# Attention scans into PSUM banks, fillers into the next product's bank, and a planner that counts the shared port

## The chip, the cores and the metric

One core of a Trainium2 chip runs the whole program. TensorE (PE; its weight loads are PEld) multiplies, VectorE (DVE), ScalarE (ACT) and GpSimd (POOL) do the element work, and SyncE (SP) issues most of the transfers. SBUF is the working memory; PSUM, eight banks of 2 KB per partition, takes the products of TensorE. The metric is the device time of one execution in microseconds (us), lower is better; a kernel's time is the median of its runs.

## What is computed

Three layers in fp32, cut to the core:

```python
# layer 1: gated linear attention, 4 x 8 heads, 768 steps, head size 48
for t in range(S):
    state = alpha[:, :, t, :, None] * state + k[:, :, t] (outer) v[:, :, t]
    y[:, :, t] = q[:, :, t] @ state
x = y as [3072 tokens, 384]
# layer 2: 8 experts, each token goes to its two best
noisy = x @ w_gate + log1p(exp(x @ w_noise)) * noise
out[token] = sum over its top 2 of weight * (relu(x @ w1[e]) @ w2[e])     # 384 -> 1024 -> 384
# layer 3: dense, leaky relu
h = out @ w_in;  result = max(0.01 * h, h) @ w_out                        # 384 -> 2048 -> 384
```

## The kernel before

**Order of the work.** No engine's order is written out by hand. `build_unit`, `build_route` and `build_experts` register steps with a `Planner` (line 70): the engine (or two to choose from), an estimated duration, what the step depends on, which buffers it takes (`Ring`s, listed at line 923 with their sizes) and a due time. `prepare` hands due times back from each step to those it waits for. `run` (line 125) keeps a clock for each engine, always issues the step that can start first by these estimates, and breaks ties by the due time. Each engine then executes its instructions in that order. `run(1)` issues until the attention is done, with phase 1 steps alone; `run(2)` issues the rest.

**Attention** goes in 24 units of 128 steps, all heads at once (`build_unit`, line 932), six units for each of the four sequences. SP loads `at` (alpha), `kq` and `nv`. On DVE `back` (line 963) scans alpha backwards into `suf` with one long scan, `forth` (969) scans forwards into `wt` in two halves, each behind a small reciprocal; then `keys` (988) multiplies k by `suf` into `kt` and `queries` (992) q by `wt` into `qp`. `suf` and `wt` lie in SBUF, three buffers each. The scans' second operand, a pattern of resets, lies in a PSUM bank `pC` (line 909). POOL multiplies the totals of alpha (`total`, 978). On TensorE `turn_k` (1000) transposes the keys into a `pM` bank, ACT copies them out (1004), `update` (1048) and `carry` (1052) add up the new state in another `pM` bank, ACT copies it to `S` (1057), and POOL decays it for the next unit (`sp`, 1039). `score` (1013) writes two banks, ACT copies them (1017), POOL masks them (1022), `within` (1069) and `across` (1076) make y in `pY`, ACT copies it (1093), and `turn_y` (1098) transposes y and multiplies by the gate weights into a `pA` bank, from which ACT copies x (1102) and DVE takes the logits (1107). The eight banks in this stage: `pA` 2, `pC` 1, `pM` 2, the scores 2, `pY` 1.

**Fillers.** Where the planner sees TensorE idle for more than 0.45 us ahead of a product, `keep_busy` (line 917) issues matmuls of the identity, so many as fit into the gap. They write to the unused end of bank `pC`.

**Routing.** After four units (one group of 512 tokens, six groups) some thirty small steps on DVE and ACT (`gate_top2`, line 177, and `build_route`, 1121) find each token's two experts and its slot, and POOL scatters the rows of x to the slots in DRAM (`x_s`), eight indirect transfers for a group (line 1191). The first two experts' first rows (`EARLY`) need groups 0 to 3 alone.

**Experts and dense layer** (`build_experts`, 649). Each product is split into three fp32r products of high and low parts. Weights come by SP and are split by ACT (`split_hi`, 464) and by DVE or POOL, whichever the planner finds free (`split_lo`, 468). Rows are loaded from `x_s` (526), transposed by TensorE into `pA` (`turn`, 600) and split by ACT (604) and DVE (609). `gemm1` (742) writes `ph`, `gemm2` (781) adds up in `py`.

Of the kernel before, what the change touches and what calls it, by code (L numbers as in the profile page):

```python
# [16 lines left out]
DRAM = bass.MemoryType.DRAM  # L17

SQ_MAX, TOT_MIN = 460.0, 1e-14
PERIOD = 6.0  # L20
RDUE = -10.0
# [6 lines left out]
RGROUPS = ((0,), (1,), (2,), (3,), (4,), (5,))  # L28
CAP = G0 + G1
GROUP2 = 384  # L30
F64B = 2
XGB = 11
# [37 lines left out]
class Planner:  # L70

    NEAR, FAR, SLACK, RATE, LAND = 0.1, 0.25, 0.8, 0.26, 2.0
    GAP, FILL, COLD, AHEAD, MARGIN = 0.45, 0.24, 0.45, 0.3, 3.0

    def __init__(self):
        self.steps, self.free, self.dma = [], dict.fromkeys("pavgs", 0.0), 0.0
        self.filler = None

    def add(self, eng, dur, fn, deps=(), use=(), takes=(), phase=1, due=1e9, lat=0.0, size=0):

        deps = list(deps)
        st = Step(eng, dur, fn, deps, list(takes), phase, due, lat, size)
        for owner, ring in use:
            deps.append(owner)
            owner.holders[ring].append(st)
        for ring in st.takes:
            ring.planned.append(st)
        self.steps.append(st)
        return st

    def prepare(self):
# [13 lines left out]
        for st in sorted(self.steps, key=lambda x: -order[x]):  # L105
            for nx in st.succ + [x for x in before.get(st, []) if order[x] > order[st]]:
                far = 0 if nx.eng == st.eng else self.SLACK
                st.due = min(st.due, nx.due - nx.longest() - far - st.lat)
        self.waiting = set(self.steps)
        self.open = [st for st in self.steps if not st.left]  # L110

    def start_of(self, st):
        t = 0.0
        for d in st.deps:
            t = max(t, d.end + (self.NEAR if d.used == st.eng[0] else self.FAR))
        for ring in st.takes:
# [8 lines left out]
    def run(self, phase, until=None):  # L125

        left = set(until) if until else None
        while left or (left is None and any(s.phase <= phase for s in self.waiting)):
            best = {}
            for st in self.open:  # L130
# [5 lines left out]
                for e in st.eng:  # L136
                    t0 = max(t, self.free[e])
# [12 lines left out]
            if e == "p" and self.filler and t0 - self.free[e] > self.GAP:  # L150
                self.filler(int((t0 - self.free[e]) / self.FILL if self.free[e] else (t0 - 1.0) / self.COLD))
# [3 lines left out]
            self.free[e] = t0 + dur  # L155
            st.t0 = t0
# [20 lines left out]
def gate_top2(nc, work, lg, noise, desc, n, tagp, res):  # L177
# [28 lines left out]

    @op(A)
    def _():
        nc.scalar.activation(t3("ln"), flat(t["u"]), AF.Ln)

    @op(V)
    def _():
        nc.vector.scalar_tensor_tensor(t3("um"), flat(t["u"]), -1.0, flat(t["ex"]), op0=OP.add, op1=OP.subtract)
# [122 lines left out]
def tile_kernel(  # L336
# [50 lines left out]
    ps2 = fctx.enter_context(tc.tile_pool(name="psum2", bufs=2, space=PSUM))  # L387
# [129 lines left out]
    scattered, late, taken = [], [], []  # L517
# [5 lines left out]
    def load_rows(e, g, j):  # L523
# [3 lines left out]
        if g == 0 and e < EARLY:  # L527
# [62 lines left out]
    XT, XP = {}, {}  # L590

    def turn(key, j):
# [5 lines left out]
        p = XP[key, j] = ps2.tile([128, KD, 128], FT, name="pA")  # L598
# [50 lines left out]
    def build_experts(t0, R, scat, last_x, ready_at, totals, acc_done, begun):  # L649
# [18 lines left out]
        def turned(key, phase):  # L668
            done = []
            for j, (o, n) in enumerate(blocks(key)):  # L670
                own = [XO[key]] if j else []
                w = add("p", 0.34, lambda j=j: turn(key, j), own + AUX.get((key, j), []),
                        use=[(GX[key + (j,)], R["xg"])] + [(x, R["XT"]) for x in own],
                        takes=[R["pA"]] + ([] if j else [R["XT"]]), phase=phase, due=tm[0] - 7 + 0.8 * j if phase == 2 else 1e9)
                if not j:
                    XO[key] = w
                hi = add("a", 0.5, lambda j=j: turned_hi(key, j), use=[(w, R["pA"]), (XO[key], R["XT"])], phase=phase)
                lo = add("v", 0.57, lambda j=j: turned_lo(key, j), [hi], use=[(w, R["pA"]), (XO[key], R["XT"])], phase=phase)
# [4 lines left out]
        def expert_weights(i, after):  # L683
# [4 lines left out]
            for m, nm in enumerate(("w1s", "w2s")):  # L688
# [175 lines left out]
        for si, (gi, f, nf) in enumerate(steps):  # L864
# [31 lines left out]
            if si == first[2 * EARLY]:  # L896
                v0 = add("v", 1.3, violations, totals, phase=2, due=tm[0] + 40)
# [6 lines left out]
    with ExitStack() as actx:  # L904
# [5 lines left out]
        scb, warm = bank[:PP, 0:HB * C + C], bank[:, HB * C + C:]  # L910
# [6 lines left out]
        def keep_busy(n):  # L917
            for _ in range(n):
                nc.tensor.matmul(warm, identf, identf, start=True, stop=True)  # L919

        plan.filler = keep_busy
# [560 lines left out]
```

## Time and profile before

| | us |
|---|---|
| median of 3 runs | 1096.68 (1092.26 to 1100.07) |
| the profiled execution | 1087.71 |
| its span, first to last instruction | 1085.9 |
| TensorE busy, of the span | 1042.8 |
| VectorE busy | 593.7 |
| ScalarE busy | 388.2 |
| GpSimd busy | 278.5 |

All rows below are of the profiled execution, and their times count from the start of its span. Busy times are averages over stages of different kinds: the attention lies at the front, and the experts and the dense layer fill the rest.

### The profile page before, as it was taken

Reading aid. Unit: us, or ns where it says so; the run is one execution under the profiler, and the core shown is the slowest. Engines: PE = TensorE matmul, PEld = TensorE weight load, DVE = VectorE, ACT = ScalarE, POOL = GpSimd, SP = SyncE. Lnnn points to the kernel's source line nnn. Section 1 sums busy time; section 2 is a strip of 40 time slices with the busy share of each in tenths; the row PEclk is TensorE's granted clock in tenths of the full one; section 3 lists DMA queues with packets and bytes.
Section 4 is the critical chain, followed back from the end, with each engine's and each line's share of the span. In section 5 each row is a group of like instructions: output and inputs, shape, how many; then the busy total and the mean of one; then the engine's idle time right before and its main releaser. Section 6 shows DMA issues by size and latency. Waiting matters only on the chain.

```text
span 1085.9 us, 18172 instructions
## 1 busy us (share of the span) xinstructions
PE 1042.8 (96%) x6839; PEld 999.2 (92%) x6839; DVE 593.7 (55%) x1218; ACT 388.2 (36%) x825; POOL 278.5 (26%) x321
## 2 busy tenths in 40 slices
PE   6999895999999999999999999999999999999997
PEld 5887775999999999999999989899999999999997
DVE  5998997223464565646574233455554545454543
ACT  3755644223354544445453222222222222212211
POOL 3466876200032253424351021410110100000000
PEclk9998997999999999999999999999999999999999
DMA  9667746413464565746567344320101100000000
GB/s 232 203 203 242 237 129 222 157 50 103 148 201 141 179 200 164 226 142 207 180 222 241 116 153 139 92 66 9 59 22 45 34 33 16 22 1 23 1 22 26
DMA packets 78917, 133.20 MB, mean 123 GB/s; under 512 B 8514, under 2 KB 56260, under 8 KB 78820
## 3 DMA queue, kind: packets, MB, share of 16 engines
q1 hardware_dynamic: 72292, 111.89, 33.2%
q0 software_dynamic: 6528, 20.06, 5.7%
q8 instruction: 56, 0.92, 0.4%
q14 instruction: 41, 0.34, 0.1%
HBM read 93.38 MB, written 38.54 MB: 121 GB/s over the span
## 4 chain that ended last, share of the span: by engine, by line
PE 87%; DVE 8%; issue 2%; DMA 1%; ACT 1%; another core or an unknown queue 1%; POOL 0%; DVEq 0%; ACTq 0%; POOLq 0%
PE py L781 39%; PE ph L742 39%; PE pA L600 2%; DVE wt L974 1%; PE pS L1013 1%; DVE suf L965 1%; PE pA L1098 1%; PE pY L1069 1%; PE pC L919 1%; PE pY L1076 1%; DVE kt L988 1%; PE pM L1048 1%; DMA xg<-y_d,gidx 1%; DVE g_z L225 0%
## 5 line engine op out<-in xcount | busy, mean ns | idle before, releaser
L766 DVE SCALAR_TENSOR_TENSOR hl<-ph,hh 128x384 fp32r<-128x384 f32 (+1 forms) x128 | 77.4, 606 | 192.3 <-ACT hh L759 186.1
L752 ACT ACTIVATE hc<-ph 128x384 f32<-128x384 f32 x128 | 63.0, 492 | 300.6 <-PE ph L742 283.3
L755 DVE SCALAR_TENSOR_TENSOR hc<-hc 128x384 f32<-128x384 f32 x128 | 71.4, 558 | 178.2 <-ACT hc L752 178.2
L759 ACT ACTIVATE hh<-ph 128x384 fp32r<-128x384 f32 (+1 forms) x128 | 68.0, 532 | 241.7 <-PE ph L742 236.0
L781 PE MATMUL py<-w2hA,hh 128*128 128x384 f32 (+1 forms) x416 | 141.5, 340 | 1.1 <-issue 1.1
L781 PE MATMUL py<-w2hB,hh 128*128 128x384 f32 (+1 forms) x416 | 141.9, 341 | 0.2 <-issue 0.2
L781 PE MATMUL py<-w2lB,hh 128*128 128x384 f32 (+1 forms) x416 | 140.5, 338 | 0.4 <-issue 0.4
L781 PE MATMUL py<-w2hB,hl 128*128 128x384 f32 (+1 forms) x416 | 140.5, 338 | 0.0
L781 PE MATMUL py<-w2hA,hl 128*128 128x384 f32 (+1 forms) x416 | 140.0, 337 | 0.0
L781 PE MATMUL py<-w2lA,hh 128*128 128x384 f32 (+1 forms) x416 | 139.9, 336 | 0.0
L742 PE MATMUL ph<-xh,w1hA 128*128 128x384 f32 (+1 forms) x384 | 136.4, 355 | 1.4 <-ACT hc L752 0.7
L742 PE MATMUL ph<-xl,w1hA 128*128 128x384 f32 (+1 forms) x384 | 134.3, 350 | 1.0 <-issue 1.0
L742 PE MATMUL ph<-xh,w1hB 128*128 128x384 f32 (+1 forms) x384 | 134.1, 349 | 0.4 <-DVE hl L766 0.4
L742 PE MATMUL ph<-xh,w1lA 128*128 128x384 f32 (+1 forms) x384 | 134.1, 349 | 0.0
L742 PE MATMUL ph<-xl,w1hB 128*128 128x384 f32 (+1 forms) x384 | 133.4, 347 | 0.0
L742 PE MATMUL ph<-xh,w1lB 128*128 128x384 f32 (+1 forms) x384 | 133.3, 347 | 0.0
L804 POOL DMA_INDIRECT xg<-y_d,gidx x48 | 46.5, 968 | 279.6 <-PE pA L600 172.7
L781 PEld LDWEIGHTS py<-w2lA,hh 128*128 128x128 f32 (+1 forms) x416 | 77.3, 186 | 2.2 <-issue 1.2
L781 PEld LDWEIGHTS py<-w2lB,hh 128*128 128x128 f32 (+1 forms) x416 | 77.6, 187 | 1.3 <-issue 0.3
L781 PEld LDWEIGHTS py<-w2hB,hh 128*128 128x128 f32 (+1 forms) x416 | 77.5, 186 | 0.8
L769 DVE TENSOR_TENSOR hl<-hc,hh 128x384 fp32r<-128x384 f32 x128 | 71.4, 558 | 12.3 <-DVE hh L761 0.5
L781 PEld LDWEIGHTS py<-w2hB,hl 128*128 128x128 f32 (+1 forms) x416 | 77.6, 187 | 0.5 <-issue 0.5
(160 smaller groups left out, 1877.3 us busy)
## 6 DMA issues: line engine op xcount, KB each, us to landing
w1s<-in_moe_w_dram SPq DMA_DIRECT2D x32, 384.0 KB
w2s<-in_moe_w_dram SPq DMA_DIRECT2D x32, 384.0 KB
kq<-in_kq_l_dram SPq DMA_DIRECT2D x24, 448.0 KB
nv<-in_v_l_dram SPq DMA_DIRECT2D x24, 256.0 KB
w1s<-in_moe_w_in_dram SPq DMA_DIRECT2D x24, 256.0 KB
w2s<-in_moe_w_out_dram SPq DMA_DIRECT2D x16, 384.0 KB
xg<-x_s SPq DMA_DIRECT2D x32, 180.0 KB
y_d<-ys SPq DMA_DIRECT2D x32, 180.0 KB
```

The costliest lines, as they stand in the source:

```text
L600: nc.tensor.transpose(p[:, d, :n], src[:n, d * 128:(d + 1) * 128], identf[:n, :n])
L742: nc.tensor.matmul(ps[:, :n], a[:, d, fo:fo + 128], x[:, d, :n], start=i == 0, stop=i == len(seq) - 1)
L752: nc.scalar.activation(hc[:, :n], ps[:, :n], AF.Copy)
L755: nc.vector.scalar_tensor_tensor(hc[:, :n], hc[:, :n], 0.01, hc[:, :n], op0=OP.mult, op1=OP.max)
L759: nc.scalar.activation(hh[:, :n], ps[:, :n], AF.Relu)
L766: nc.vector.scalar_tensor_tensor(hl[:, :n], ps[:, :n], 0.0, hh[:, :n].bitcast(FT), op0=OP.max, op1=OP.subtract)
L769: nc.vector.tensor_sub(hl[:, :n], HT[si, "hc"][:, :n], hh[:, :n].bitcast(FT))
L781: nc.tensor.matmul(py[:n, :], h[:, o:o + n], w[:, f % 2, :], start=(f == 0 and i == 0), stop=(f == nf - 1 and i == 2))
L804: nc.gpsimd.indirect_dma_start(out=yg, out_offset=None, in_=y_d[0:rows, :], in_offset=bass.IndirectOffsetOnAxis(ap=gidx[:, c, kk:kk + 1], ...
L919: nc.tensor.matmul(warm, identf, identf, start=True, stop=True)
L965: nc.vector.tensor_tensor_scan(rev(d["suf"][:, :]), rev(d["at"][:, 1:NW + 1]), rev(d1b), 0.0, OP.mult, OP.add)
L974: nc.vector.tensor_tensor_scan(d["wt"][:, i * hc:(i + 1) * hc], d["at"][:, i * hc:(i + 1) * hc], scb[:, 0:hc], 0.0, OP.mult, OP.add)
```

## The change

- `suf` and `wt` become PSUM banks, one each (`pF`, `pT`; rings 3 to 1). To make room `pM` goes from two banks to one and `pA` from two to one; after the attention a bank `pB` stands beside `pA`, and the row transposes take them in turn.
- `total` moves from POOL to DVE.
- Fillers no longer write to `pC`. `turn_k`, `score` and `within` have a `room` function that takes the step's own bank, and the fillers go there, from when the bank is free.
[...]
- In phase 1 the low parts of the weights are split by DVE alone. The due time of the first expert's row transposes and splits is set to 0 (`TURN`), without being handed back.
- In group 3's routing, runs of up to 10 steps on one engine become one planner step (`FUSED`, `RUN`).
- Gate weights and noise are due at 0 (`LCD`) and not after the first unit; the gate's `um` is computed ahead of its `ln`; the check `violations` waits for an expert product; 12 buffers for rows and not 11; the first row loads get an explicit dependence on the scatters; some estimates of the planner change.

```diff
+LCD = 0.0
+XGB = 12
+FUSED = ((3,),)
+RUN = 10
+TURN = 0.0
...
-                    t0 = max(t, self.free[e])
+                    t0 = max(t, self.free[e], self.port if st.port and e in "vg" else 0.0)
...
-            if e == "p" and self.filler and t0 - self.free[e] > self.GAP:
-                self.filler(int((t0 - self.free[e]) / self.FILL if self.free[e] else (t0 - 1.0) / self.COLD))
+            if e == "p" and st.room:
+                gap = t0 - max(self.free[e], self.room_of(st))
+                if gap > self.GAP:
+                    st.room(int(gap / (self.FILL if self.free[e] > 1.5 else self.COLD)))
...
+        if first_rows not in awaited:
+            for other in scattered:
+                if not (first_rows and other in late):
+                    tc.add_manual_dep(ins.ins, other.ins.name, SYNC, reason="the rows of every choice are in their slots")
...
+                bk = bank_of[key, j] = "pB" if phase == 2 and len(bank_of) % 2 else "pA"
...
-                AUX[i].append([hi, add("vg", dict(v=0.87, g=1.8), lambda en, m=m: split_lo(i, m, en), [hi],
-                                       use=[(fe, R[nm]), (WO[i], R["W"])], phase=phase)])
+                AUX[i].append([hi, add("vg" if phase == 2 else "v", dict(v=0.87, g=1.8) if phase == 2 else 0.87, lambda en="v", m=m: split_lo(i, m, en), [hi],
+                                       use=[(fe, R[nm]), (WO[i], R["W"])], phase=phase, port=True)])
...
-                nc.tensor.matmul(warm, identf, identf, start=True, stop=True)
+                nc.tensor.matmul(area, identf, identf[:, 0:area.shape[1]], start=True, stop=True)
...
-            at=5, kq=4, nv=5, suf=3, wt=3, kt=4, qp=4, pM=2, kN=2, pS=1, pT=1, ar=2, am=2, sp=2, S=2, pY=1, xt=XTB,
-            scr=1, pA=2, xg=XGB, XT=2, W=NA + NB, ...
+            at=5, kq=4, nv=5, suf=1, wt=1, kt=4, qp=4, pM=1, kN=2, pS=1, pT=1, ar=2, am=2, sp=2, S=2, pY=1, xt=XTB,
+            scr=1, pA=1, pB=1, xg=XGB, XT=2, W=NA + NB, ...
...
-                d["suf"] = work.tile([PP, NW], FT, name="suf", bufs=3)
+                d["suf"] = psum.tile([PP, NW], FT, name="pF", bufs=1)
...
-                    d["wt"] = work.tile([PP, NW], FT, name="wt", bufs=3)
+                    d["wt"] = psum.tile([PP, NW], FT, name="pT", bufs=1)
...
-                nc.gpsimd.tensor_mul(tots[:, u, :], d["sv"][:, :, 0], d["at"][:, NW + 1:NW + 1 + HP])
+                nc.vector.tensor_mul(tots[:, u, :], d["sv"][:, :, 0], d["at"][:, NW + 1:NW + 1 + HP])
...
+            def room_k(n=0):
+                d["pk"] = psum.tile([128, HP, PP], FT, name="pM", bufs=1)
+                keep_busy(d["pk"][:, 0, :], n)
...
-        rc = add("g", 6.0, route_consts, due=at_unit(2))
-        ld = add("s", 0.14, load_consts, lat=2.5, due=at_unit(1))
+        rc = add("g", 3.05, route_consts, due=0.0)
+        ld = add("s", 0.8, load_consts, size=0.13, due=LCD)
```

## Rows read from the trace of the kernel before

**Rows 1.** Busy time by stage: stretch, its length, then busy us (instructions) of each engine
```profile
20.00:165.00 145.00, 135.40 (x1727) 115.07 (x1722) 132.48 (x330) 87.00 (x209) 95.86 (x130) 0.95 0.68 207
165.00:180.00 15.00, 3.62 (x18) 2.85 (x18) 11.86 (x31) 6.16 (x13) 9.51 (x8) 0.63 0.77 254
180.00:1086.00 906.00, 893.49 (x5032) 871.60 (x5030) 440.87 (x842) 290.87 (x595) 169.37 (x160) 1.00 0.33 105
```

**Rows 2.** Timeline of the handover: start, us, engine, line, instruction
```profile
115.30 0.23 ACT L201 ACTIVATE g_ex<-lg 128x32 f32<-128x32 f32 x1
...
144.34 0.17 DVE L1184 SCALAR_TENSOR_TENSOR si<-pk,g_cm 128x8 uint32<-128x8 f32 x1 [0.18 <-DVE pk L1180]
...
151.04 1.16 PE L1013 MATMUL pS<-qp,kt 48*128 48x128 f32 x16
...
152.72 2.04 PE L1098 MATMUL pA<-turn_w,xt 128*128 128x112 f32 x16
...
163.87 1.15 PE L1098 MATMUL pA<-turn_w,xt 128*128 128x112 f32 x8
...
166.53 1.02 PE L600 MATMUL pA<-identf,xg 128*128 128x128 f32 x6 [1.51 <-DMA xg<-x_s]
...
175.38 0.90 PE L600 MATMUL pA<-identf,xg 128*128 128x128 f32 x3 [7.83 <-DVE xl L609]
...
178.56 0.67 PE L742 MATMUL ph<-xh,w1hA 128*128 128x384 f32 x1
```

**Rows 3.** Timeline of the first units
```profile
7.44 4.80 PE L919 MATMUL pC<-identf 128*128 128x128 f32 x22 [7.44 <-DVE wt L974]
...
7.86 0.35 SPq L1219 DMA_DIRECT2D wgn<-in_wgp_l_dram  x1
...
18.38 1.29 PE L1013 MATMUL pS<-qp,kt 48*128 48x128 f32 x16
```

**Rows 4.** Waits in the attention: us in total, times, longest
```profile
POOL turn_w L1231 <- DMA wgn<-in_wgp_l_dram: 13.1, 1, 13.1
...
DVE suf L965 <- PE pC L919: 5.0, 1, 5.0
...
DVE pC L973 <- PE pC L919: 4.5, 3, 3.0
```

**Rows 5.** Chain that ended last, pieces of one unit's products: start, us
```profile
39.63 1.07 PE pA L1098 x8
...
44.28 0.45 PE pM L1048 x14
44.72 1.01 PE pY L1076 x16
```

**Rows 6.** Groups of instructions, 0 to 180 us: count, busy us, mean ns, idle before
```profile
L965 DVE TENSOR_TENSOR_SCAN suf<-at,pC 112x512 f32<-112x512 f32 x24 | 28.8, 1207 | 7.2 <-PE pC L919 5.0 <-DMA at<-in_al_l_dram 2.3
...
L988 DVE TENSOR_TENSOR kt<-kq,suf 112x512 f32<-112x512 f32 x24 | 17.8, 743 | 0.0
...
L973 DVE RECIPROCAL pC<-suf 112x2 f32<-112x2 f32 x48 | 8.1, 168 | 4.8 <-PE pC L919 4.5
...
L265 DVE SCALAR_TENSOR_TENSOR g_z<-g_oh,g_z 128x32 f32<-128x32 f32 x6 | 4.0, 674 | 0.2
...
L468 DVE TENSOR_TENSOR w1lB<-w1s,w1hB 128x768 fp32r<-128x768 f32 x2 | 1.9, 952 | 0.4 <-issue 0.4
...
L609 DVE TENSOR_TENSOR xl<-pA,xh 128x384 fp32r<-128x384 f32 x3 | 1.6, 547 | 0.0
...
L288 DVE RECIPROCAL g_ws<-g_ws 128x4 f32<-128x4 f32 x5 | 0.8, 163 | 0.0
```

**Rows 7.** Line 988, window 100 to 160: shortest, median, longest ns
```profile
L988 DVE TENSOR_TENSOR kt<-kq,suf x8: 666/684/831, 104.9 to 149.5; 112x512 f32<-112x512 f32 x8
```

**Rows 8.** Timeline: a POOL split and the DVE step beside it
```profile
127.11 1.82 POOL L468 TENSOR_TENSOR w1lA<-w1s,w1hA 128x768 fp32r<-128x768 f32 x1
...
127.77 2.38 DVE L265 SCALAR_TENSOR_TENSOR g_z<-g_oh,g_z 128x32 f32<-128x32 f32 x1
```

More of the change, by code (lines that the diff above doesn't have):

```diff
@@ L31 @@
 F64B = 2
-XGB = 11
 XTB = 3
@@ L70, with add @@
 class Planner:
-    NEAR, FAR, SLACK, RATE, LAND = 0.1, 0.25, 0.8, 0.26, 2.0
-    GAP, FILL, COLD, AHEAD, MARGIN = 0.45, 0.24, 0.45, 0.3, 3.0
+    NEAR, FAR, SLACK, RATE, LAND = 0.1, 0.25, 0.8, 0.25, 2.0
+    GAP, FILL, COLD, AHEAD, MARGIN = 0.45, 0.24, 0.42, 0.3, 3.0
     def __init__(self):
-        self.steps, self.free, self.dma = [], dict.fromkeys("pavgs", 0.0), 0.0
-        self.filler = None
-    def add(self, eng, dur, fn, deps=(), use=(), takes=(), phase=1, due=1e9, lat=0.0, size=0):
+        self.steps, self.free, self.dma, self.port = [], dict(p=1.5, a=2.1, v=1.8, g=1.8, s=0.8), 0.0, 0.0
+    def add(self, eng, dur, fn, deps=(), use=(), takes=(), phase=1, due=1e9, lat=0.0, size=0, own=1e9, port=False, room=None):
         deps = list(deps)
         st = Step(eng, dur, fn, deps, list(takes), phase, due, lat, size)
+        st.port, st.room = port, room
+        st.own = own
         for owner, ring in use:
@@ L108, in prepare @@
                 st.due = min(st.due, nx.due - nx.longest() - far - st.lat)
+        for st in self.steps:
+            st.due = min(st.due, st.own)
         self.waiting = set(self.steps)
@@ L155, in run @@
             self.free[e] = t0 + dur
+            if st.port and e in "vg":
+                self.port = t0 + dur
             st.t0 = t0
@@ L896, in build_experts @@
             if si == first[2 * EARLY]:
-                v0 = add("v", 1.3, violations, totals, phase=2, due=tm[0] + 40)
+                v0 = add("v", 1.3, violations, totals + [S1[first[EARLY]]["g1"]], phase=2, due=tm[0] + 40)
                 v1 = add("p", 0.4, flag_sums, [v0] + acc_done, takes=[R["pA"]], phase=2, due=tm[0] + 50)
@@ L1025, in build_unit @@
             if not last:
-                tk = add("p", 0.48, turn_k, use=[(kk, R["kt"])], takes=[R["pM"]], due=b + 0.6)
+                tk = add("p", 0.48, turn_k, use=[(kk, R["kt"])], takes=[R["pM"]], due=b + 0.6, room=room_k)
                 ck = add("a", 0.44, copy_k, use=[(tk, R["pM"])], takes=[R["kN"]])
             sel = []
-            sc = add("p", 1.09, score, use=[(kk, R["kt"]), (qq, R["qp"])], takes=[R["pS"], R["pT"]], due=b + 2.4)
+            sc = add("p", 1.09, score, use=[(kk, R["kt"]), (qq, R["qp"])], takes=[R["pS"], R["pT"]], due=b + 2.4, room=room_s)
             for i in range(2):
@@ L1110, in build_unit @@
             cy = add("a", 0.5, copy_y, [done], use=[(w0, R["pY"])], takes=[R["xt"]])
-            ty = add("p", 0.8, turn_y, [consts_in], use=[(cy, R["xt"])], takes=[R["pA"]], due=b + PERIOD + TYD)
+            ty = add("p", 0.98, turn_y, [consts_in], use=[(cy, R["xt"])], takes=[R["pA"]], due=b + PERIOD + TYD)
             cx = add("a", 0.39, copy_x, use=[(ty, R["pA"])], takes=[R["xg"]])
@@ L1246, in tile_kernel @@
         plan.run(1, core + totals)
-        plan.filler = None
     with ExitStack() as mctx:
```

113 lines of the change are left out of this document (72 added, 41 removed).

## The prediction

> **What bounds the kernel now.** I read the busy times by stage first, then the timeline where the attention hands over to the experts, the first units, the waits, and last the groups of instructions on DVE. From 180 us to the end TensorE is busy 893.5 of 906 us at full clock [rows 1]. The change gives that stage neither fewer nor cheaper products, so I keep its length, and all that can be won lies ahead of it. The attention, 20 to 165 us, keeps two engines near their limit: TensorE 135.4 and DVE 132.5 of 145 us [rows 1]. Then TensorE stands nearly idle: the last `turn_y` ends at 163.87 + 1.15 = 165.0 and the first expert product starts at 178.56 [rows 2]. These 13.5 us are the handover. In it TensorE is busy 3.6 of 15 us, at a granted clock of 0.63 [rows 1].
>
> The third loss is the start. The first score runs only at 18.38 [rows 3], because 22 filler matmuls, 4.80 us of them from 7.44, write to the bank that holds the scans' operand: the second backward scan waits 5.0 us for TensorE, the reciprocals of `forth` 4.5 us in three waits, the longest 3.0 [rows 4]. POOL's copy of the gate weights waits 13.1 us for their late load [rows 4].
>
> Which of the two engines sets the pace? From the first score (18.38) to the last (151.04) a unit takes 132.7 / 23 = 5.77 us. In the chain the products from 39.63 to 44.72 + 1.01 = 45.73 follow each other without a gap, and they are one unit's worth and a second update of 0.45: 5.65 us for a unit [rows 5]. First and last units of the four sequences lack some products, about half a unit a sequence, so the attention's floor on TensorE is 24 x 5.65 - 4 x 2.8 = 124 us, 5.2 a unit. The pace stands 0.6 us a unit above it, so DVE and the waits between engines set it, and TensorE takes over if they lose more than 13 us.
>
> **The change, part by part.**
>
> *Fillers out of `pC`.* The waits of rows 4 vanish: 5.0 + 4.5 = 9.5 us of DVE time, of which 8.0 in the start. The fillers now stand ahead of their own product on TensorE's queue and delay nothing but it. If the plan sees a gap that isn't there, they cost what they last, some 0.2 us each by 4.80 / 22; I take nothing for that.
>
> *Constants first.* Two transfers now go ahead of the first alpha on SP; an issue holds the queue 0.35 us [rows 3] and they share the transfer engines, so the first scan starts 0.7 to 1.5 us later, I take 0.9. In return POOL is not held by the 13.1 us wait; the first masks stand behind it. I count the start as -8.0 + 0.9 = -7.1 us, and 1.5 us for the later filler wait.
>
> *Products free of the port.* `kt` takes 743 ns in the mean [rows 6] and 666 at its shortest [rows 7]: 24 x 0.077 = 1.8 us beside POOL work; for `qp`, the same kind, 1.2: together -3. In the routing one step of two inputs, `g_z` (L265), took 674 ns in the mean [rows 6], and once 2.38 us just where a POOL split of 1.82 us ran [rows 8]. Against 0.17 for a small step that is 0.5 x 6 = 3 us for this line alone; with a dozen two-input steps in a group the bounds are 3 and 36, I take 12. Masks, decay and scatters stay on POOL, splits leave it, and the plan knows the port: half goes, -6. POOL also gets its masks done sooner; with 95.9 of 145 us busy [rows 1] it is not the bound.
>
> *PSUM as output and input of DVE.* No row shows such a scan. A reciprocal into PSUM takes 168 ns, one into SBUF 163 [rows 6]: 5 ns x 72 scans = 0.4 us. `xl`, which reads PSUM, takes 547 ns for 384 columns [rows 6]; the shortest `kt`, scaled from 512 columns, 666 x 0.75 = 500 [rows 7]. For the 72 instructions that now read PSUM (`kt`, `qp`, `tots`) that is at most 72 x 0.047 = 3.4 us, at least 0, as part of the time is fixed and doesn't scale. I take 1 in all.
>
> [...]
>
> *`total` on DVE.* 24 small multiplies; by the reciprocal's 168 ns 4.0 us, less where they overlap their neighbours, at least 1.5: +3. *Splits on DVE.* An instruction takes 952 ns [rows 6]; five of the first expert's eight ran on POOL, 4.8 us. They are due late and mostly fall behind the last scan, beside TensorE's tail: +2. *Fused routing* gives up the overlap of dependent steps for one group: +1. `violations` moves into the expert stage, where DVE is busy 441 of 906 us [rows 1]: 0; without that cover it would cost under 1 us.
>
> *One bank each.* `suf` and `wt` are used by DVE alone now, so their rings add no wait for another engine. With one `pM`, `turn_k` waits on TensorE's queue until ACT has copied the state of the unit before, and the next `score` stands behind it; with one `pA`, a `turn_y` waits for ACT's copy and the logits of the one before. The room is there if the plan spreads them over 5.7 us; I take 0, and a rival below holds the price.
>
> Sum for the attention: -7.1 - 1.5 - 3 - 6 + 1 + 3 + 2 + 1 = -10.6, its last `turn_y` ends near 154. From a first score near 11 the TensorE floor would end it at 11 + 124 = 135 and a short tail, so TensorE doesn't take this back.
>
> *Handover.* Group 3's routing ran from 115.30 to 144.34, 29 us, as its steps were strewn between the units' [rows 2]. Fused, some 25 steps of 0.2 us and a few changes of engine are 10 to 13 us. With the earlier pace its slots are known near 120 and not 144. Before, the first rows stood on TensorE 22 us after that (166.53); so now at 142. The three transposes then waited up to 7.83 us for `xl` [rows 2], which stood behind routing and splits; their due time is now 0. With one `pA` bank the blocks go one after the other, each two products' lengths and two copies, about 2.2 us: ready at 149, ahead of 154. What is late next is the low part of the first weights: one split of 0.95 us and waits. I put the first expert product at 156, 22.5 us earlier than 178.56. If the cover goes (rows after 154), each us of lateness costs one. The explicit dependence on the scatters stands in SP's queue; behind it wait weight loads for the second expert, not needed for some 25 us.
>
> `pB`, 12 row buffers and the changed estimates touch the stage from 180 us, where TensorE hardly waits: 0.
>
> Made against the profiled execution the time is 1087.7 - 22.5 = 1065. The median of the runs shown stands 9.0 us above that execution (1096.7); keeping the distance, 1074.
>
> **Rivals.**
>
> A. *The handover stays.* The rows are still late (scatters of group 3 behind masks on POOL, or loads behind others on SP), so the 13.5 us remain and only 10.6 are won: 1086. For it: 22 us from slots to rows. Against: 24 us of lead.
>
> B. *DVE fills up again.* The port costs as much as before (masks and scatters remain), `total` costs 4.0, the splits 4.8, PSUM 3.4. Then 8.6 won by fillers and start stand against 12.2, the handover gives some 4: 1096, no change. For it: DVE at 132.5 of 145. Against: rows 7 and 8, where POOL splits did the longest harm.
>
> C. *One `pA` bank in lockstep: slower.* Before, two `turn_y` ran back to back, 16 matmuls in 2.04 us from 152.72 [rows 2]; with one bank the second waits for logits that stand on DVE behind a scan of 1.21 [rows 6] and a product, up to 2 us. TensorE has only 0.6 us a unit to spare. It decides from 22.5 / 24 = 0.94 us a unit; at 1.5 us the attention loses 36: 1096.7 - 22.5 + 36 = 1110. Against: the planner knows each ring and moves other products in.
>
> **How the numbers follow.** Forecast 0.69 (1074, its own range 1060 to 1084), A 0.12, B 0.11, C 0.08. Runs of this kernel differ by 0.7%, so 1% (11 us) is about what can be told from no change. Faster by over 1%: the forecast and half of A, 0.75; within 1%: the other half and B, 0.17; slower 0.08. Range 1058 to 1093: below, the other half of the port's 12 us goes too (6), the handover closes (2) and half of the pace's 16 us above TensorE's floor is found (8), 16 in all; above, it reaches past A most of the way to B.
>
> **What would show it.** Right: no wait of DVE for a filler, first score near 11, `kt` and `qp` never over 0.72 us, group 3 from `g_ex` to `si` in under 15 us, last `turn_y` ends at 150 to 158, first expert product within 4 us of it. Wrong: TensorE waits for logits or ACT's copies ahead of `turn_y` or `turn_k` over 0.5 us a unit, scans longer than 1.25 us, or row loads that land after the last `turn_y`.

## The result, and the profile after

The changed kernel takes 1083.63 us (median of 12 runs, 1077.02 to 1088.99) beside 1094.43 of the kernel before (12 runs on the same chip, 1088.88 to 1100.30): a ratio of 0.990, 95% interval 0.987 to 0.993. That is 10.8 us less; the prediction had 22.5 less (1074), with a range of 1058 to 1093. The profiled execution of the changed kernel took 1084.43, with a span of 1082.6; that of the kernel before had 1085.9.

The times differ from one set of runs to the next, and each set of the experiments ran on a chip of its own. The kernel before took 1094 here, 1095 and 1091 on two of the other chips, 1080 on two more, and on one of the last two the same change gives a ratio of 0.982. Both kinds of chip are needed to see what the change does, and each number below says where it is from. That it is the chip, and not something else that differed between the sets, is the shortest way to say it and not shown.

First the busy time of the changed kernel by stage, in the columns of [rows 1]; the stages are split at the end of the last `turn_y` and at the first expert product:

```profile
20.00:157.00 137.00, 124.16 (x1584) 103.67 (x1580) 118.32 (x334) 79.34 (x192) 73.18 (x96) 0.95 0.68 205
157.00:165.00 8.00, 3.53 (x13) 2.40 (x13) 5.14 (x20) 4.16 (x10) 4.73 (x5) 0.54 0.97 351
165.00:1083.00 918.00, 897.33 (x5035) 875.04 (x5035) 448.49 (x856) 294.89 (x601) 178.28 (x166) 0.99 0.34 106
```

The attention is 8 us shorter than the 145 of [rows 1], the gap behind it 8 us long and not 13.5. But the last stage, which had 906 us for the same products, now has 918. The timeline of the start and the handover, which answers to [rows 2] and [rows 3]:

```profile
8.46 0.72 PE L1049 MATMUL pS<-qp,kt 48*128 48x128 f32 x8
...
105.07 0.23 ACT L219 ACTIVATE g_ex<-lg 128x32 f32<-128x32 f32 x1 [0.29 <-DVE lg L1147]
...
115.49 0.19 DVE L1203 TENSOR_TENSOR acc<-run,acc 128x32 bf16<-128x32 bf16 x1
...
123.28 0.19 PE L1212 MATMUL pA<-ot,tri 128*128 128x32 bf16 x1
...
130.73 0.22 DVE L1224 TENSOR_TENSOR sel<-g_oh,pos 128x64 f32<-128x64 f32 x1
...
131.38 0.17 DVE L1234 SCALAR_TENSOR_TENSOR si<-pk,g_cm 128x8 uint32<-128x8 f32 x1 [0.18 <-DVE pk L1230]
...
155.55 1.15 PE L1138 MATMUL pA<-turn_w,xt 128*128 128x112 f32 x8 [2.41 <-issue]
158.62 0.90 PE L625 MATMUL pA<-identf,xg 128*128 128x128 f32 x3 [1.93 <-issue]
160.70 0.90 PE L625 MATMUL pA<-identf,xg 128*128 128x128 f32 x3 [1.18 <-DVE xl L634]
163.27 0.90 PE L625 MATMUL pA<-identf,xg 128*128 128x128 f32 x3 [1.67 <-issue]
163.96 0.85 PE L625 MATMUL pB<-identf,xg 128*128 128x128 f32 x3
164.75 0.69 PE L770 MATMUL ph<-xh,w1hA 128*128 128x384 f32 x1
```

The first score comes 9.9 us earlier than in [rows 3], the first expert product 13.8 us earlier than in [rows 2]. Yet the whole span is 3.3 us shorter. The other 10.5 us are lost again later, some 6 of them here, where TensorE gets 70 matmuls done in the 20 us from 180 and in the kernel before 108 (timeline of the changed kernel, all engines):

```profile
185.66 0.49 ACT L787 ACTIVATE hh<-ph 128x384 fp32r<-128x384 f32 x1 [1.73 <-PE ph L770]
...
188.41 0.34 PE L770 MATMUL ph<-xh,w1lA 128*128 128x384 f32 x1
...
192.48 0.98 POOL L1244 DMA_INDIRECT x_s<-xg,si  x1 [0.30 <-issue]
...
192.78 0.52 PE L809 MATMUL py<-w2hA,hl 128*128 128x384 f32 x1
...
195.88 0.87 ACT L787 ACTIVATE hh<-ph 128x384 fp32r<-128x384 f32 x2 [9.72 <-remote]
...
197.01 0.69 PE L770 MATMUL ph<-xh,w1hB 128*128 128x384 f32 x1 [3.71 <-DVE hl L794]
```

The block of products that ACT waits for is done at 188.41 + 0.34; ACT starts on it at 195.88, and "remote" says that its wait ends in no event of the core's engines. In between POOL issues the last of 14 indirect writes that began at 175.47, one about every 1.3 us. A second wait of that kind, 12.0 us, stands near 680 beside a row of gathers. TensorE runs dry in both, and when it comes back its products are slower for a while (0.52 us each from 197.50 to 200, where they took 0.34 at 188.41; the granted clock is 0.50 from 197 to 200): in the mean the granted clock is 0.80 from 180 to 200 and 0.83 from 680 to 700.

Last the groups on DVE from 0 to 180 us, in the columns of [rows 6]:

```profile
L1001 DVE TENSOR_TENSOR_SCAN pT<-at,pC 112x256 f32<-112x256 f32 x48 | 33.4, 696 | 1.6
L992 DVE TENSOR_TENSOR_SCAN pF<-at,pC 112x512 f32<-112x512 f32 x24 | 29.4, 1223 | 2.4 <-DMA at<-in_al_l_dram 2.2
L1019 DVE TENSOR_TENSOR qp<-kq,pT 112x512 f32<-112x512 f32 x24 | 16.3, 680 | 0.0
L1015 DVE TENSOR_TENSOR kt<-kq,pF 112x512 f32<-112x512 f32 x24 | 16.2, 676 | 0.0
L1000 DVE RECIPROCAL pC<-pF 112x2 f32<-112x2 f32 x48 | 8.3, 174 | 0.3
...
L1147 DVE TENSOR_REDUCE lg<-pA 128x16 f32<-128x64 f32 x24 | 5.2, 217 | 12.1 <-ACT xg L1142 9.4 <-remote 1.6 <-PE pA L1138 1.0
...
L1005 DVE TENSOR_TENSOR tots<-pF,at 112x4 f32<-112x4 f32 x24 | 3.6, 152 | 0.0
```

No scan and no reciprocal waits for a filler any more, a scan into PSUM takes 16 ns longer (1223 against 1207 in [rows 6]), and `kt` is at 676 where it had 743. What stands against it is 12.1 us of waiting ahead of the logits. So two things had to be explained: why the pace of the units did not improve here ((142.55 - 8.46) / 23 = 5.83 us a unit, 5.77 before), and what these late starts of ACT are.

### The profile page after: what moved, and what is told of

Same layout as the page of the kernel before. It is cut to its first block, busy times and chain, and to the rows that moved or that the text cites. A ratio compares the mean times of both kernels' runs of the same rounds, so it can differ in the third digit from the quotient of the medians.

```text
span 1082.6 us, 18035 instructions
## 1 busy us (share of the span) xinstructions
PE 1042.7 (96%) x6811; PEld 997.1 (92%) x6811; DVE 588.3 (54%) x1242; ACT 389.2 (36%) x826; POOL 264.3 (24%) x296
## 4 chain that ended last, share of the span: by engine, by line
PE 90%; DVE 3%; DMA 2%; another core or an unknown queue 2%; ACT 1%; issue 1%; SPq 0%; POOL 0%; DVEq 0%; ACTq 0%; POOLq 0%
PE py L809 39%; PE ph L770 38%; PE pA L1138 2%; PE pS L1049 2%; PE pY L1109 2%; PE pY L1116 2%; PE pB L625 1%; PE pA L625 1%; PE pM L1084 1%; PE pM L1032 1%; PE pM L1088 1%; DMA w2s<-in_moe_w_dram 1%; DMA xg<-y_d,gidx 1%; DMA nv<-in_v_l_dram 1%
## 5 line engine op out<-in xcount | busy, mean ns | idle before, releaser
L809 PEld LDWEIGHTS py<-w2hA,hh 128*128 128x128 f32 (+1 forms) x416 | 77.8, 187 | 2.8 <-issue 2.0
L770 PEld LDWEIGHTS ph<-xh,w1hA 128*128 128x128 f32 x384 | 73.0, 190 | 7.7 <-ACT hc L780 5.0
```

The source lines that it names most:

```text
L770: nc.tensor.matmul(ps[:, :n], a[:, d, fo:fo + 128], x[:, d, :n], start=i == 0, stop=i == len(seq) - 1)
L809: nc.tensor.matmul(py[:n, :], h[:, o:o + n], w[:, f % 2, :], start=(f == 0 and i == 0), stop=(f == nf - 1 and i == 2))
```

## The experiments

**First set, a chip of 1080.** The first theory was that a row of indirect transfers holds up the signals by which TensorE tells ACT that a product is done; so I doubled the fills (the writes to slots that no token took), and in another kernel spread the writes. Two more kernels priced the banks.

Twice the fills:

```diff
-                  for i in range(NF)]
+                  for i in list(range(NF)) * 2]
```

> Six more indirect writes to x_s (each of the six fills runs a second time, the same rows with the same data). Theory, burst: while POOL issues indirect transfers back to back, TensorE's completion signals to ACT are held until the last of them has landed; ACT then waits for a product that is long done. Each write takes 1.28 us of POOL, so the stall after 188 us ends some 7.7 us later than in the changed kernel (hh at 195.88 there, about 203.5 here), TensorE is busy 7 us less between 180 and 220, and the whole time is 6 to 8 us longer. Rival, something else is late there (weights, ACT's own work, code): the stall stays where it is, and the time moves by under 2 us.

Measured: 1059.42 us in one run, beside 1080.32 before. There is no stall at all: TensorE is busy 20.00 of 20 us between 180 and 200, though POOL issues twenty indirect writes, one about every 1.3 us (at 172.72, 174.31 and so on to 180.72, each 0.30 us behind the one before), and is busy with ten instructions, 9.19 us, in this stretch. The theory as it stood falls: a row of writes alone does not hold anything. The rival, a stall that stays where it is, falls with it.

The writes spread:

```diff
+    def paced(ins):
+        if newest:
+            tc.add_manual_dep(ins.ins, newest[-1].ins.name, SYNC, reason="not before TensorE is here")
...
+        paced(ins)
...
-        filled = [add("g", 1.29, lambda i=i: fill(i, last_x[0]["x"]), [fl], ...
+        filled = [add("g", PACE, lambda i=i: fill(i, last_x[0]["x"]), [fl], ...
```

> The last 14 indirect writes (six fills, eight scatters of group 5) are spread over the first products of the experts: each waits for the newest second product that was planned before it, one about every 2.2 us in place of 1.28. Theory, burst: TensorE is busy 19 or more of 20 us between 180 and 200 (14.4 in the changed kernel), ACT waits there for no product over 4 us, and the time is 4 to 6 us shorter, about 1078. Rival, something else is late there: the stall stays, the time stays at 1083 or grows, as the rows of the third block of experts come 10 us later.

Measured: 1060.58, ratio 0.982 (0.980 to 0.984). That would have looked like a confirmation, had the first kernel not shown that on this chip there is no stall to take away.

The scans back in SBUF and two banks each for `pM` and `pA`:

```diff
-                d["suf"] = psum.tile([PP, NW], FT, name="pF", bufs=1)
+                d["suf"] = work.tile([PP, NW], FT, name="suf", bufs=SB)
...
-            at=5, kq=4, nv=5, suf=1, wt=1, kt=4, qp=4, pM=1, kN=2, pS=1, pT=1, ar=2, am=2, sp=2, S=2, pY=1, xt=XTB,
-            scr=1, pA=1, pB=1, xg=XGB,
+            at=5, kq=4, nv=5, suf=SB, wt=SB, kt=4, qp=4, pM=2, kN=2, pS=1, pT=1, ar=2, am=2, sp=2, S=2, pY=1, xt=XTB,
+            scr=1, pA=2, pB=1, xg=XGB,
...
-                bk = bank_of[key, j] = "pB" if phase == 2 and len(bank_of) % 2 else "pA"
+                bk = bank_of[key, j] = "pA"
```

> The changed kernel with suf and wt in SBUF again (rings of three), and the two banks given back: two for pM and two for pA, row transposes in pA alone. The rest of the change stays. Theory, one bank costs what the scans' banks save: DVE waits for logits under 4 us (12.1 in the changed kernel), group 3 goes from g_ex to si in under 18 us (26.3), and TensorE waits for no copy ahead of turn_y; against it kt and qp take 0.74 us again (0.68) and the routing's two-input steps meet masks a little more. Attention ends within 2 us of 156.7, the first expert product comes at 160 to 163 as two banks turn the rows faster, the time is 1080 to 1084. Rival, the banks were worth it: DVE's work grows by more than 5 us, the first expert product comes after 167, time over 1087.

Measured: 1065.79, ratio 0.988 (0.986 to 0.990). Logits wait 3.9 us for ACT's copies, group 3 takes 21.7 us, and the first expert product comes at 156.62, but the rows behind it are late: TensorE is busy 15.73 of 20 us between 160 and 180. The time is shorter than both theory and rival had it, as they were made against the 1083.6 of the result.

The scans back in SBUF, one bank each as in the change:

```diff
-                d["suf"] = psum.tile([PP, NW], FT, name="pF", bufs=1)
+                d["suf"] = work.tile([PP, NW], FT, name="suf", bufs=SB)
...
-                    d["wt"] = psum.tile([PP, NW], FT, name="pT", bufs=1)
+                    d["wt"] = work.tile([PP, NW], FT, name="wt", bufs=SB)
```

> The changed kernel with suf and wt in SBUF again (rings of three), but one bank each for pM and pA as in the change: the banks of the scans stay empty, so this prices the place of the scans alone. If a product free of the port is worth what the trace says: kt and qp 0.68 to 0.74 us, 48 x 0.06 = 3 us of DVE's work back, scans 1.1 us less, steps of the routing as in the change; attention ends 1 to 4 us later than 156.7, time 1084 to 1088. If DVE is not what sets the pace (its waits for logits take up what it gains or loses), the time stays within 2 us of 1083.6.

Measured: 1066.63, ratio 0.988 (0.986 to 0.991). The groups of this kernel on DVE, 0 to 190 us:

```profile
L1016 DVE TENSOR_TENSOR kt<-kq,suf 112x512 f32<-112x512 f32 x24 | 18.7, 780 | 0.0
L1020 DVE TENSOR_TENSOR qp<-kq,wt 112x512 f32<-112x512 f32 x24 | 17.5, 731 | 0.0
...
L1006 DVE TENSOR_TENSOR tots<-suf,at 112x4 f32<-112x4 f32 x24 | 7.4, 318 | 0.0
```

The line of `tots` by itself, with its shortest, median and longest in ns:

```profile
L1006 DVE TENSOR_TENSOR tots<-suf,at x24: 132/152/1640, 15.0 to 142.3; 112x4 f32<-112x4 f32 x24
```

The same product in the changed kernel, with one operand in PSUM (the first line of the result's execution, the second and third of the one that follows below):

```profile
L1005 DVE TENSOR_TENSOR tots<-pF,at x24: 135/153/157, 5.8 to 140.0; 112x4 f32<-112x4 f32 x24
L1015 DVE TENSOR_TENSOR kt<-kq,pF x24: 672/674/682, 6.8 to 131.5; 112x512 f32<-112x512 f32 x24
L1019 DVE TENSOR_TENSOR qp<-kq,pT x24: 671/680/687, 7.4 to 133.8; 112x512 f32<-112x512 f32 x24
```

The same little product that takes 157 ns at most from PSUM takes up to 1640 with both operands in SBUF. The last two kernels differ by the two banks and where the rows are turned, and their times are within 0.8 us of each other: in the time the banks are worth nothing that shows. Their courses differ all the same. With one bank group 3 takes 33.0 us and the first product comes at 164.51, with two 21.7 and 156.62; what the two banks win at the handover is lost behind it.

**Second set, the other chip of 1080.** Since all four had been quicker than the changed kernel had seemed, it ran again unaltered, and so did the kernel before.

> The changed kernel, nothing altered. Its four variants so far came to 1059 to 1067 beside 1080 of the kernel before, and their profiles show the granted clock at 1.00 from 20 to 100 us, where the changed kernel's own profile has 0.86 to 0.88 in two stretches. Theory, one execution: that profile holds waits of its own (clock, a stall after 188 us), and another execution of the same program ends its last turn_y at 145 to 148, starts the expert products at 155 to 158 and has no stall after 188; the ratio is 0.980 to 0.987. Rival, the variants are better kernels: last turn_y at 156 to 158, first expert product at 164 to 166, stall of 3 us or more after 188, ratio 0.990.

Measured: 1060.84, ratio 0.982 (0.981 to 0.984). Its timeline:

```profile
98.85 0.23 ACT L219 ACTIVATE g_ex<-lg 128x32 f32<-128x32 f32 x1 [0.29 <-DVE lg L1147]
...
123.88 0.17 DVE L1234 SCALAR_TENSOR_TENSOR si<-pk,g_cm 128x8 uint32<-128x8 f32 x1 [0.18 <-DVE pk L1230]
...
135.11 1.16 PE L1049 MATMUL pS<-qp,kt 48*128 48x128 f32 x16
...
145.46 1.15 PE L1138 MATMUL pA<-turn_w,xt 128*128 128x112 f32 x8 [0.70 <-ACT xt L1133]
...
148.71 0.52 PE L625 MATMUL pA<-identf,xg 128*128 128x128 f32 x3 [2.11 <-DVE g_um L227]
...
156.18 0.69 PE L770 MATMUL ph<-xh,w1hA 128*128 128x384 f32 x1
```

> The kernel before, nothing altered, for a profile beside the others of this call. Theory, one execution: the kernel before has the same course in every execution, since its pace is set by DVE: last turn_y near 165, first expert product near 178 as in rows 2; then the 1.5% between this set's times and the first one lie after 180 us. Rival: it moves by as much as the changed kernel, last turn_y at 157 or earlier.

Measured: 1079.04 in one run. Its last `turn_y` and first expert product:

```profile
162.84 1.04 PE L1098 MATMUL pA<-turn_w,xt 128*128 128x112 f32 x8
...
176.29 0.67 PE L742 MATMUL ph<-xh,w1hA 128*128 128x384 f32 x1
```

On this chip the change does what was predicted: the first expert product comes 20.1 us earlier, and 18.8 of these are left at the end of the span (1077.3 to 1058.5). The first product of the kernel before moved by 2.3 us only, as the theory had it. The pace of the units, which did not improve on the chip of the result, does here: (135.11 - 8.14) / 23 = 5.52 us a unit, and 5.72 in the kernel before.

Where do the two executions of the changed kernel part? Both issue the same order and are never 0.4 us apart up to the scores at 50.1. The timeline of the one of the result:

```profile
49.89 1.20 POOL L1244 DMA_INDIRECT x_s<-xg,si  x1 [4.28 <-DVE pC L1000]
50.16 1.16 PE L1049 MATMUL pS<-qp,kt 48*128 48x128 f32 x16
...
53.54 0.60 ACT L1053 ACTIVATE ar<-pS 128x512 f32<-128x512 f32 x1 [3.34 <-PE pA L1138]
...
55.16 2.00 PE L1049 MATMUL pS<-qp,kt 48*128 48x128 f32 x16
```

And of the one of this set:

```profile
49.86 1.20 POOL L1244 DMA_INDIRECT x_s<-xg,si  x1 [4.28 <-DVE pC L1000]
50.14 1.16 PE L1049 MATMUL pS<-qp,kt 48*128 48x128 f32 x16
51.39 0.60 ACT L1053 ACTIVATE ar<-pS 128x512 f32<-128x512 f32 x1 [1.22 <-PE pS L1049]
...
53.01 1.16 PE L1049 MATMUL pS<-qp,kt 48*128 48x128 f32 x16
```

The same scores end at 51.3 in both. Here ACT copies them 0.1 us later, there 2.2 us later, just when the first indirect writes of the program are on their way. TensorE then has nothing to do for 1.92 us, its granted clock falls to 0.57 in the mean from 55 to 57, and the next scores take 2.00 us and not 1.16. DVE starts late too: its logits run at 54.34, 1.6 us behind the `turn_y` that ended at 51.67 + 1.04, and that wait also ends in "remote" (the 1.6 in the result's groups above). So it looks like the same thing as at 188 us, it is not ACT's alone, and it does not happen on this chip.

The start alone (undone are: scans in SBUF, two banks, `total` on POOL, splits on either engine, no `port` in the plan, no runs, no due time of 0; the 12 row buffers, the order of `um`, the dependence of the row loads and the new estimates stay):

```diff
-FUSED = ((3,),)
-TURN = 0.0
+FUSED = ()
+TURN = 1e9
...
-                    t0 = max(t, self.free[e], self.port if st.port and e in "vg" else 0.0)
+                    t0 = max(t, self.free[e], 0.0)
```

> The changed kernel with all undone but the start: scans to SBUF rings of three, two banks each for pM and pA, total on POOL, splits on either engine, no port in the plan, nothing fused, rows without a due time of 0. What stays is fillers in the next product's bank and the constants first. By the prediction's terms this keeps -8.6 of -22.5: first score at 9 to 11, DVE waits for no filler, last turn_y near 157, first expert product near 170, ratio 0.991 to 0.993. Rival, the start is slack that the pace of DVE swallows: first expert product at 176 or later, ratio 0.996 to 1.0.

Measured: 1076.71, ratio 0.997 (0.996 to 0.999), 3 us. The first score is at 9.27, 7.7 us earlier than in the kernel before on this chip; the last `turn_y` ends at 160.73, 3.2 us earlier, and the first product comes at 175.47, 0.8 us earlier. The rival was right in its ratio, and nearly in the first product. The start's lead is lost in the pace, which is (148.38 - 9.27) / 23 = 6.05 us here and 5.72 in the kernel before. That DVE swallows it, as the rival had it, is not shown: between 100 and 140 DVE is busy 35.7 of 40 us, less than the 39.3 of the kernel before, while TensorE's clock is at 0.70, and at 0.96 there. Why the clock fell there was not followed up.

No runs in group 3's routing:

```diff
-FUSED = ((3,),)
+FUSED = ()
```

> The changed kernel with group 3's routing in single steps (no runs). In the profiles of the variants group 3 went from g_ex to si in 25 us with runs of steps, 26.3 in the changed kernel, 29 before: the runs took 10.4 us of it, the rest is the wait for the bank of position and a place in the queues. Theory, the runs give little as the rows still have to wait for scatters that are spread by their due times: group 3 takes 27 to 32 us, the rows come 0 to 3 us later, time within 3 us of after_again. Rival, the runs bring the rows forward: first expert product 5 us or more later than in after_again, time 4 us or more longer.

Measured: 1065.38, ratio 0.986 (0.984 to 0.989), 4.5 us more than the changed kernel. Group 3 takes 28.1 us and not 25.0, and the first product comes 1.8 us later. The time is the rival's, the timeline the theory's: the runs are worth something, and more than the handover shows.

**Third set, a chip of 1095.** These three came to the kind of chip of the first result and compare with its 0.990 (0.987 to 0.993). A plan in which the steps marked `port` (the masks, the decay, the low-part splits, the routing steps on DVE) may overlap on DVE and POOL, and in which the splits of phase 1 may go to either:

```diff
-                    t0 = max(t, self.free[e], self.port if st.port and e in "vg" else 0.0)
+                    t0 = max(t, self.free[e], 0.0)
...
-                AUX[i].append([hi, add("vg" if phase == 2 else "v", ...
+                AUX[i].append([hi, add("vg", dict(v=0.87, g=1.8), lambda en, m=m: split_lo(i, m, en), [hi],
```

> The changed kernel with a plan that does not know the port: masks, decay and two-input steps are placed beside each other as before, and the first expert's splits may run on POOL. All else stays (scans in PSUM, one bank each, total on DVE, runs, rows due at 0). Theory, the plan's part is small once products and tots read PSUM: kt and qp stay at 0.68 us, the routing's two-input steps grow by 2 to 5 us in sum, first expert product 157 to 161 (156.2 in after_again), time 2 to 4 us longer than 1060.8. Rival, the plan's part is the larger: first expert product later than 164, time over 1067.

Measured: 1084.50, ratio 0.990 (0.987 to 0.993). `kt` and `qp` keep their 676 and 680 ns, as both theories need; from 0 to 180 us the routing's groups on DVE add up to 47.2 us where the changed kernel of the result has 38.5, but DVE's splits to 5.7 where it has 13.0. The first product comes at 167.33, 2.6 us later, and the time is the same. So the plan and the splits moved off POOL do take 8.7 us off the routing, and 7.3 us of splits on DVE pay for it; no gain in the time can be shown.

No due time of 0 for the first rows:

```diff
-TURN = 0.0
+TURN = 1e9
```

> The changed kernel with no due time of 0 for the first rows' transposes and splits (they are due by the products that need them, as before). In after_again the first transpose runs at 148.71, 2.1 us behind the last turn_y, and the first product 7.5 us later; in before_again the product came 13.5 us behind the last turn_y. Theory, the due time is what shortens the handover: the first product comes 10 us or more behind the last turn_y, 159 or later, time over 1064. Rival, the handover is shorter because group 3's rows are there early: first product within 2 us of 156.2, time within 2 us of 1060.8.

Measured: 1082.05, ratio 0.987 (0.984 to 0.990). The first product comes 10.5 us behind the last `turn_y` (8.0 in the changed kernel): by these two profiles the due time shortens the handover by some 2.5 us, and the time doesn't show it.

Only `suf` in PSUM, two `pA` banks:

```diff
-                    d["wt"] = psum.tile([PP, NW], FT, name="pT", bufs=1)
+                    d["wt"] = work.tile([PP, NW], FT, name="wt", bufs=SB)
...
-    ps2 = fctx.enter_context(tc.tile_pool(name="psum2", bufs=1, space=PSUM))
+    ps2 = fctx.enter_context(tc.tile_pool(name="psum2", bufs=2, space=PSUM))
```

> The changed kernel with only suf in PSUM; wt goes back to SBUF (ring of three) and its bank to a second pA, with the row transposes in pA alone. The scan of wt costs 10 ns less each, 0.5 us in all; qp takes 0.73 in place of 0.68, 24 x 0.05 = 1.2 us more; tots stays at 0.15. Theory, the second pA bank is worth more than that: logits wait under 1 us in all, group 3 goes from g_ex to si in under 20 us (25.0 in after_again), the three row blocks are turned 2 to 3 us sooner, first product 153 to 155, time 1057 to 1060. Rival, one bank costs nothing as the plan has spread what uses it: time 1060 to 1064.

Measured: 1080.79, ratio 0.986 (0.983 to 0.989). Group 3 takes 28.1 us: a second `pA` bank doesn't shorten it here. This run also has both places of an operand side by side: `kt`, from PSUM, takes 668 ns in the mean, `qp`, from SBUF, 743. The interval overlaps the others', so of the three none is shown to be better or worse than the change.

But all three show the late starts. The waits of ACT that end in "remote", 160 to 230 us and then 600 to 720 us, in the changed kernel of the result (us in total, times, longest):

```profile
ACT hh L787 <- remote: 9.7, 1, 9.7
...
ACT hc L780 <- remote: 12.0, 1, 12.0
```

The same in the first of these three:

```profile
ACT hh L787 <- remote: 14.4, 2, 11.2
...
ACT hc L780 <- remote: 9.2, 1, 9.2
```

The other two have 6.6 and 11.5, 5.2 and 10.6; the kernel before, 4.5 and 5.5 at the longest. In the eight profiles from the chips of 1080 no wait of ACT in these stretches ends so.

**Fourth set, a chip of 1091.** A test of whether the transfers are a cause or only stand by: the last writes and all gathers of the last stage held back, as in the second kernel of the first set and with this besides:

```diff
-            nc.gpsimd.indirect_dma_start(out=yg, out_offset=None, in_=y_d[0:rows, :],
-                                         in_offset=bass.IndirectOffsetOnAxis(ap=gidx[:, c, kk:kk + 1], axis=0))
+            paced(nc.gpsimd.indirect_dma_start(out=yg, out_offset=None, in_=y_d[0:rows, :],
+                                               in_offset=bass.IndirectOffsetOnAxis(ap=gidx[:, c, kk:kk + 1], axis=0)))
```

> The changed kernel with the last 14 indirect writes and all gathers of the last stage held back: each waits for the newest second product planned before it, and the plan counts 2.2 us for one in place of 1.29. It computes the same. The kernel before came to 1080 in two sets of runs and to 1094 and 1095 in two others. In the five profiles of the slower sets ACT has waits that end in no event of its own core, of 5 to 12 us, where POOL issues eight or more indirect transfers back to back (185 to 196 us, 674 to 685 us); in the eight profiles of the faster sets there is none. Should this set be of the slower kind (before near 1095): theory, the back-to-back transfers hold TensorE's signals there, so no such wait over 4 us is left at 180 to 200 and 670 to 690, and the ratio falls from 0.990 to 0.980 to 0.984; rival, they only stand beside another cause: the waits stay, ratio 0.988 or more. Should it be of the faster kind (before near 1080): no such wait is there to be taken away, and both say a ratio of 0.981 to 0.985.

Measured: 1060.48 beside 1090.79, ratio 0.974 (0.970 to 0.977). Busy time by stretch of the changed kernel of the result, in the columns of [rows 1]:

```profile
180.00:200.00 20.00, 14.42 (x70) 13.18 (x69) 4.00 (x9) 3.08 (x6) 10.41 (x11) 0.80 0.43 153
...
680.00:700.00 20.00, 15.04 (x74) 14.71 (x74) 10.32 (x21) 5.36 (x11) 7.61 (x8) 0.83 0.31 87
```

And of this one:

```profile
180.00:200.00 20.00, 20.00 (x116) 20.00 (x115) 3.89 (x8) 4.42 (x9) 8.86 (x10) 1.00 0.34 120
...
680.00:700.00 20.00, 20.00 (x118) 19.97 (x117) 12.97 (x26) 7.15 (x14) 6.22 (x6) 1.00 0.32 97
```

No "remote" wait is left in these two stretches; one of 2.5 us stays in the attention, whose scatters were not held back. That is what the theory says of a chip of this kind: where the transfers are spaced the waits are gone, where they are not one stays. It is not a proof, as the changed kernel itself did not run on this chip. The ratio is the lowest of all, by more than the theory had put on it (0.980 to 0.984), though the time is only what the changed kernel takes on a chip of 1080. Part of it is not the late starts at all. From the first product to the end of the span this kernel takes 1059.5 - 162.38 = 897.1 us, and the changed kernel 902.3 even on the second chip, where it has none of them; there TensorE is busy 17.33 of the 20 us from 620 to 640, and here, with the gathers planned otherwise, 20.00. How much of the step from 0.990 to 0.974 is the chip's stays open.

## Why the prediction was right, and where not

**In sum.** Faster was right, and 1083.6 lies in the range. The size came to half on the chip of the result and to most of it elsewhere: on the chip of the second set the first expert product stands at 156.18, forecast 156, and the median is 18.7 us less, forecast 22.5. But that agreement is luck. On that chip the last `turn_y` ends 17.3 us earlier (163.88 to 146.61), forecast 10.6, and the handover shrinks by 2.8, forecast 12: two errors of opposite sign. On the chip of the result the 10.8 us won are rival A's 10.6 almost to the number, but by another way than A's: the attention gave 8.3 and the handover 5.5, and the stage behind them lost again what A had not won.

**Start, forecast -8.6 with the later filler wait: right at its place, not shown in the sum.** The fillers' waits are gone and the first score is 8.9 to 9.9 us earlier; the constants cost the first scan 0.2 us at most. But alone this gives 3 us in time and 0.8 at the first product. I counted what is won at the start as won at the end, though I had said that DVE and the waits between engines set the pace; alone, the lead went into a slower pace (6.05 us a unit, and 5.72 in the kernel before).

**Products free of the port, forecast -3 and -6: right in kind, too small.** Every `kt` and `qp` lies between 671 and 687 ns on the second chip, and their sum fell from 36.9 to 32.5 us. The routing's groups fell from 55.8 to 43.1 us on that chip and from 52.6 to 38.5 in the first two profiles: the full 12 that I had worked out and then halved. On the other side stand the splits, forecast +2: the first expert's eight on DVE take 10.2 us in the result's profile and 8.6 on the second chip, where I had 0.95 each. And the place of the scans did for `tots` what I had not counted: it would cost 7.4 us from SBUF and costs 3.6 from PSUM (forecast 3.0). Scans back in SBUF make the kernel 5.8 us slower (1066.6 against 1060.8, on chips where the kernel before takes 1080); this is the largest single part that the runs show. DVE's own work is only part of the way: with three buffers each the plan also orders the work otherwise, and group 3 takes 33.0 us in place of 25.0.

The rows show where the difference lies: with the scans in SBUF a product of two SBUF operands goes up to 1640 ns (`tots`; `kt` up to 1285), the same one with one operand in PSUM never over 157 (`kt` never over 682). One `kt` from SBUF takes 1.20 us, from 104.55, beside a mask on POOL of 1.03 us from 105.21; one from PSUM, in the result's execution, takes 0.68, from 85.77, with a mask of 0.63 from 85.81 wholly beside it. That DVE and POOL share a port is what I assumed, in the plan's `port` as in the prediction's -3 and -6; no run shows a port, only these durations.

**PSUM as operand, forecast +1: right.** The scans grew from 61.7 to 62.7 us and the reciprocals from 8.1 to 8.5 on the second chip; the shortest `kt` takes 672 ns from PSUM and 666 from SBUF, 6 ns.

**One bank each, forecast 0: right in the time.** With scans in SBUF one bank or two differ by 0.8 us, and rival C falls. Logits do wait on the first chip (12.1 us), but the same program with the same bank has only 2.1 on the second: so the bank alone does not make them wait.

**Handover, forecast -12: wrong.** The gap went from 13.5 to 8.0 us, on the second chip from 12.4 to 9.6. The step that failed is "some 25 steps of 0.2 us and a few changes of engine are 10 to 13 us". The run of steps on DVE did end 10.4 us after `g_ex` (115.49), but the products for the positions ran at 123.28, behind others in TensorE's queue, and the next step on DVE at 130.73, behind scans: 15 us for the way over TensorE and ACT and back, and 12.4 on the second chip. So group 3 took 26.3 and 25.0 us, not 10 to 13, and the sign of under 15 failed. The run took 10.4 us, but here the changes of engine waited behind other work: 7.6 us from the end of the run to those products and 7.3 from their end to DVE's next step. The slots were known at 123.88 on the second chip, forecast 120, only because group 3 began 11.7 us earlier than in the kernel before on this chip. The rows then came 24.8 us after them, forecast 22, and so not ahead of the last `turn_y` but behind it, as rival A had it in part.

**The stage from 180 us, forecast 0: wrong on the first chip.** It lost 10.5 us of the 13.8, with the clock that fell in the waits (0.80 in the mean from 180 to 200, 0.83 from 680 to 700); on the second chip 1.3 of 20.1. The clock of 1.00 in [rows 1] hides that the kernel before had such waits too, of 4.5 us near 198 and of 5.5 near 692. Why it loses less to the same 14 writes was not settled.

## What to carry to other kernels

Here a product that read one operand from PSUM was not only a little faster in the mean (`kt` 676 ns, and 743 in [rows 6]), it had no long cases (682 ns at most, and up to 1285 from SBUF), and it is the long cases that cost (`tots` from SBUF: 152 ns in the median, 318 in the mean); look at shortest and longest, not at the mean. Do not count what is won ahead of a stage as won at its end before a run shows it: 7.7 us at the first score were 0.8 at the first expert product. Where engines start late beside a row of indirect transfers, try to space the transfers by waits on TensorE's own progress: with the writes alone spaced it cost nothing that shows where there are no such waits (1060.6 beside 1060.8, on the two chips of 1080), and with the gathers spaced too no such wait was left in the spaced stretches on a chip that has them.

## What was unexpected of the hardware

In three of the five sets, that of the result, that of 1095 and, in its attention, that of 1091, ACT waits up to 12.0 us on end while POOL issues indirect transfers back to back, and once begins 7.1 us after the product that it waits for (195.88 against 188.41 + 0.34). In the two sets of 1080 the same program shows nothing of it, not with twenty writes in a row either. What differs between the sets, whether it is the chip itself or what else ran beside the kernel, and whether it is the signal or the product that is held, these traces don't show.
